# Fetches of `in` issued by POOL instead of SP, a refitted order table, and set fetches put ahead of the store in front of them

## Chip, core and metric

The kernel runs on one core of one Trainium2 chip. The metric is the device time of one execution in microseconds. The core's engines are TensorE (PE, with its weight loads PEld), VectorE (DVE), ScalarE (ACT), GpSimd (POOL) and SyncE (SP); SP only issues transfers here.

## The reference

A gated delta-rule attention is followed by two feed-forward layers (FFNs) over the same 3072 tokens:

```
for t in range(768):                       # 4 batches x 8 heads, head size 40
    y[t]  = r[t] @ state
    Sa    = state @ a[t]
    state = state * w[t] - outer(Sa, b[t]) + outer(v[t], k[t])
x   = y as (3072, 320)
x   = relu(x @ w_in)**2 @ w_out            # hidden 2048
p   = domain_probs / sum                    # 4 experts
out = sum over e of p[:, e] * (relu(x @ w1[e]) @ w2[e])   # hidden 1024 each
```

## The kernel before

**Two halves.** The first half computes the attention and the first FFN. The second half computes the four experts.

**First half.** The 768 positions are cut into 24 steps of 64, two steps to a block (12 blocks). The steps of block k are 2k (even) and 2k+1 (odd). Within a step the recurrence is solved in closed form, so that most of a step is done without the state. Its pieces, by the names that the profile shows:

- `in` (b, k and a of a step, 768 KB) is fetched by `load_in` into one of three buffers. POOL scales it in place three times (L520, L512, L520), once `P`, `q` and `s` are there (DVE). `wd`, `r`, `rf`, `v` and `xv` are smaller inputs; all fetches are issued on SP's queue.
- `pm` (PE L545, L547) multiplies a and b; ACT copies it to `mb`, SP stores that to `md` in DRAM (L563). When both steps of the block have done so, SP loads the block's matrix as `mu` (L791).
- `t` is the inverse of 32x32 triangles, 62 short instructions on DVE, each of which needs the one before it (`tmp` L808, `t` L811). Then one copy turns the layout (`mu` L818, on ACT from block 1 on), SP stores it to `td` (L823) and fetches it back transposed as `t11` and `TT` in eight transfers (L832).
- `py` (PE L679, "merge1"), `pt` (L691, "merge2"), `ptx` (L714), `px` (L637), `pys` (L726) and `pst` (L754) use the inverse and the state. DVE applies masks to `ptx` (L718, into `xv`) and adds the state to `pys` (L733, L734); POOL makes the new state `ST` and the output `y`.
- The first FFN of a block is 16 units: eight matmuls into `h` (L317), three ACT passes, one DVE pass (`gl`, L878), six matmuls into `py` of the FFN (L322 to L326). Units of an earlier block fill PE between the pieces of the recurrence.

**What sets the order there.** Every piece is an operation with an engine, a due time, its dependencies and the buffers that it takes. `Schedule.run` goes over them with a table of costs, takes on each engine the ready operation of the lowest due time, and then writes out one fixed order. Each engine runs its list in that order, and an instruction that waits holds back all that stand behind it on its engine. The due times come from `DUE` and `LEAD`; `DELAY`, `COLD` and `STAY` steer the choice; `TIMES` and `MOVE` hold the costs.

**Second half.** 96 steps on PE, one expert's quarter by one 256-token pair at a time. `Beside` hands the side work out to the steps by due step (`due`), a budget of engine time in each step, and a least distance in steps between operations that need each other on different engines (`lag`). A set is one quarter of an expert's weights: `set_load` fetches it (`wm` L1066, `wr` L1067), DVE and ACT split it into high and low parts in the buffers `w` and `z`, and `set_store` stores these to `wsd` (L1104) for a later fetch by POOL. While an expert runs, the next one's four sets are made one after the other in the same buffers. `prev` makes each set's load wait for the store of the set in front of it:

```
l = job("sp", 0.9, set_load, n, deps=prev, after=after, due=D[0])
...
if store:
    return [job("sp", 1.8, set_store, s, deps=lo, lag=0, due=D[4])]
return lo + [d]
```

Of the kernel before, what the change touches and what calls it, by code (L numbers as in the profile page):

```python
# [14 lines left out]
B, H, S, D = 4, 8, 768, 40  # L15
# [27 lines left out]
def sub(base, dims):  # L43
# [2 lines left out]

DUE = dict(block=63.76, step=[98.3, -158.9, 2.4, -355.2, -9], invert=[-219.9, -0.6, -157.6], ffn=0.2, w=[-205.6, 1.33])
LEAD = dict(  # L50
    ld_wd=894.9, ld_in=421.6, scan=77.5, m=303, t_load=135.5, t=345.2, t_out=384.9, ld_r=-259.7, ld_xv=-166,
    vm=93.4, f=84.3, kbt=47.4, x=66.9, merge=66.1, tx=131.2, ys=374.4, yq=75.2, x1=185.5,
    split=112.7,
)
DELAY = dict(PE=0.21, ACT=0, DVE=0, POOL=0, SP=0.53)


class Schedule:

    COLD = 54.3  # L60
    STAY = 20.28
    SAME = 0.033

    TILING = dict(vm=1, f=1, tx=1, x=2, ys=2, m=3, merge1=4, merge2=4)
# [1 line left out]
    AFTER = dict(l1=0.10, l2=0.12, kbt=0.12, s=0.12, tx=0.10, ys=0.10, x=0.09, vm=0.11, m=0.0, f=0.01,  # L66
                 merge1=0, merge2=0, w_pe=0.1)
    TIMES = dict(
        sq0=(.32, .38), sq1=(.32, .40), sq2=(.31, .38), sq3=(.33, .41), a_xv=(.41, .41), fx=(.38, .37), s_xv=(.335, .32),
        kbtc=(.47, .57), mc=(.42, .52), xc=(.40, .49), w_abs=(.30, .41), w_low=(.23, .35), w_hi=(.28, .38),  # L70
        t2=(.76, .76), y2=(.72, .73), fc=(.25, .35), sc=(.47, .58), tt=(.98, 1.08), x1h=(.73, .83), q1=(.30, .40),
        y1=(.31, .42), g01=(.12, .21), vmm=(.66, .70), txm=(.55, .59), rs=(.86, .93), rq=(.88, .93), P=(.62, .70),
# [2 lines left out]
        m=(.58, .65), vm=(.985, 1.12), kbt=(.41, .6), tx=(.775, .94), f=(.62, .67), merge1=(.62, .69), merge2=(.62, .69),  # L75
        s=(.44, .62), kb=(1.18, 1.25), yq=(.70, .74), scale_a=(1.22, 1.27), yf=(.41, .45), te=(.95, .9), yg=(.16, .2),
        y1d=(.28, .30),
    )
    MOVE = dict(
        ld_in=(.43, 2.85, 1.67), ld_r=(.42, .94, 1.45), ld_rf=(.45, .6, 1.65), ld_v=(.45, 1.0, 1.3), ld_wd=(.43, 1.08, 1.35),  # L80
        ld_xv=(1.28, .55, 1.9), mo=(.46, .33, .91), ti=(.46, .28, 1.35), tl=(.58, 1.44, 1.62), to=(.70, 1.05, 1.19),
        tx1=(.74, .35, .95), w_ld=(.45, .61, 1.65), y1o=(.45, 2.05, .69),
    )
# [1 line left out]
        DVE=("P", "t", "x1l", "sq", "w_clamp", "w_shift", "w_sign", "w_pow", "w_mul"),  # L85
        POOL=("scale_a", "kb", "yq", "yf", "y1d", "yg"),
# [19 lines left out]
    def run(self):  # L106
# [37 lines left out]
        while len(order) < len(ops):  # L144
            best = None
            for eng in self.ENGINES:
                first, found = 1e18, []
                for n, t in ready[eng].items():
                    t = earliest(n, t, eng, first + DELAY[eng])
                    if t is not None:  # L150
                        first = min(first, t)
                        found.append((t, n))
                if found and (best is None or first < best[0]):
                    due = lambda n: ops[n][2] + (self.STAY if eng == "PE" and self.TILING.get(n[0], 0) != tiling else 0)
                    _, n, t = min((due(n), n, t) for t, n in found if t <= first + DELAY[eng])
                    best = first, n, t
# [5 lines left out]
            if eng == "PE":  # L162
# [27 lines left out]
class Beside:  # L190
# [77 lines left out]
def tile_delta_rule_moe(  # L268
# [15 lines left out]
    pe, act, dve, pool, sp = nc.tensor, nc.scalar, nc.vector, nc.gpsimd, nc.sync  # L284
# [44 lines left out]
    op = sch.op  # L329
# [77 lines left out]
    def attention(s, tt):  # L407
        k, hb = divmod(s, 2)
        d = st[s] = {}
        T, S, f, sd = TT[hb], SS[hb], FF[hb], ST[hb]  # L410
        last = s + 2 >= nsteps
        both = lambda *n: [(x, s, h) for x in n for h in range(2)]
        o = lambda *x: x[:1] + (s,) + x[1:]
# [22 lines left out]

        def load_in():
            d["in"] = ap3.tile([128, 8, 192], F32, tag="in", name=f"in{s}")
            sp.dma_start(d["in"], kba[s])

        def load_w():
            if s == 1:
# [20 lines left out]
        def load_xv():  # L463
# [4 lines left out]
        one = lambda tag, bufs, rel, alt: [(alt, 1, rel) if s == 1 else (tag, bufs, rel)]  # L468
        op(o("ld_wd"), "SP", load_w, tt - LEAD["ld_wd"], [], prev=("ld_wd", s - 1), lat=2.7,
           alloc=one("wd", 1, [o("P", 1)], "xl"))  # L470
        op(o("ld_in"), "SP", load_in, tt - LEAD["ld_in"], [], prev=("ld_in", s - 1), lat=4.3,
           alloc=[("in", 3, both("kbt", "m") + [o("vm")] + [o("a_xv", h, j) for h in range(2) for j in range(2)])])
        op(o("ld_r"), "SP", load_r, tt - LEAD["ld_r"], [], prev=("ld_r", s - 1), lat=2.7, alloc=[("r", 1, [o("vm")])])
        op(o("ld_rf"), "SP", load_rf, tt - LEAD["ld_xv"], [], prev=("ld_rf", s - 1), lat=2.7, alloc=[("rf", 2, [o("f")])])
# [306 lines left out]
    mdd, x1 = {}, {}  # L781
# [202 lines left out]
    items = [divmod(i, NF1) for i in range(units, NF1 * nblk)]
    ffn = []
# [329 lines left out]
    job = plan.job  # L1315
    NP = NF1 + 2

    done = {}
    for P in range(NPAIR):
        k, e = 2 * P, NPW * P  # L1320
        D = {0: (-50, -15, -13, -12, -10, -7, -8, -4, -2, 0, 1), 1: (-11, -9, -10, -8, -1, 1, 1, 3, 4, 5, 5)}.get(
            P, tuple(e + d for d in (-7, -5, -5, -4, -1, -3, -2, -1, 0, -1, 0)))
# [34 lines left out]
        job("sp", 0.45, x_store, P, 6, 7, deps=b6 + [("st", P, 0)], due=e + 5, key=("st", P, 6))  # L1357

    def prepare(s, D, after, rnd, store, prev, single=False):
        n = s.n  # L1360
        l = job("sp", 0.9, set_load, n, deps=prev, after=after, due=D[0])
        w = [job(rnd, 0.36, set_round2, s, i, deps=[l], lag=2, due=D[2], after=s.free) for i in range(2)]
        lo = [job("dve", 0.41, set_low2, s, i, deps=w[i:i + 1], due=D[4]) for i in range(2)]

        def part(x, y, deps, due, after, lag=1):
            r = [job(rnd, 0.05 + (y - x) / 960, set_round, s, c, x, y, deps=deps, due=due[0], after=after, lag=lag) for c in range(2)]
            q = job("dve", 0.07 + (y - x) / 960, set_rest, s, x, y, deps=r[1:], due=due[1])
            lows = [(max(x, a), min(y, b)) for a, b in ((0, 384), (384, 768), (768, 896)) if max(x, a) < min(y, b)]
# [12 lines left out]
        return lo + [d]

    homes, spare = list(range(NPW)), NPW
    prev = []
    for n in range(NPW):
        s = Set(n, homes[n], 3 * homes[n] + 4 - NP)
        D = ((-14, -18, -10, -9, -7), (-9, -10, -4, -2, -2), (-8, -5, 2, 2, 1), (-7, -1, 1, 1, 2))[n]
        prepare(s, D, -NP - 1, ("dve", "act"), False, [], True)
    for e in range(NE - 1):
        for i in range(NPW):  # L1390
            n = NPW * (e + 1) + NPW - 1 - i
            b = PER * e + (4 if e == 0 else 0) + 5 * i
            prev = prepare(Set(n, spare, b), tuple(b + d for d in ((0, 8, 8, 8, 8) if e else (-2, 0, 5, -7, 0))), b, ("act",), i < NPW - 1, prev)
# [3 lines left out]
    for G in range(NPAIR, NE * NPAIR):  # L1397
        e, i = divmod(G, NPAIR)
# [4 lines left out]
    i = -NP  # L1403
# [131 lines left out]
```

## Time and profile before

| | us |
|---|---|
| three runs | 1464.42, 1474.74, 1477.5 |
| their median | 1474.74 |
| profiled execution, whole | 1474.95 |
| its span in the trace | 1473.2 |
| PE busy | 1381.4 (94%) |
| DVE busy | 1082.5 (73%) |
| ACT busy | 785.1 (53%) |
| POOL busy | 207.8 (14%) |

The span is the time from the first to the last instruction in the trace; 1.75 us of the execution lie around it. Busy times are sums over instructions; where PE's matmuls overlap, the union is counted. The granted clock of PE is given as a share of 2.4 GHz: 1.00 is that level, and a stretch in which it was partly at the other level (1.2 GHz) shows a value in between.

### The profile page before, as it was taken

What the parts mean: (1) busy time and instruction counts of PE and PEld (TensorE: products, weight loads), DVE (VectorE), ACT (ScalarE), POOL (GpSimd) and SP (SyncE); (2) the same over time, 40 slices, a digit from 0 to 9 for tenths busy, and PEclk for the clock granted to TensorE, in tenths of its full rate; (3) what the DMA queues carried; (4) which work ended last, traced back from release to release, by engine and by line L of the source; (5) the groups of instructions that cost most, each with busy time, mean ns of one, the idle gap of its engine ahead of it and who ended that gap; (6) DMA issues with size and microseconds to landing.
All of it is one profiled execution on the core that took longest, in us unless ns stands there. A gap on an engine that the chain in (4) does not pass through costs nothing.

```text
span 1473.2 us, 39713 instructions
## 1 busy us (share of the span) xinstructions
PE 1381.4 (94%) x16072; PEld 1312.5 (89%) x16072; DVE 1082.5 (73%) x2664; ACT 785.1 (53%) x1933; POOL 207.8 (14%) x327
## 2 busy tenths in 40 slices
PE   4698999989999999999989999999999999999998
PEld 3476888888888888898989999999999999999998
DVE  7889868778788687686648556667667776866665
ACT  5486767777777676686667445533223333322221
POOL 4120311312312312221000000100001000010000
PEclk9989989999999899998999999999999999999999
DMA  8465342442543433433142344565435244344220
GB/s 248 112 196 173 91 119 63 135 124 68 136 127 74 124 110 102 119 81 80 27 150 92 117 182 172 196 224 229 154 141 200 80 190 183 125 131 168 112 93 37
DMA packets 154679, 194.61 MB, mean 132 GB/s; under 512 B 97536, under 2 KB 118272, under 8 KB 152192
## 3 DMA queue, kind: packets, MB, share of 16 engines
q1 hardware_dynamic: 147584, 140.76, 31.2%
q0 software_dynamic: 6912, 51.32, 9.5%
q8 instruction: 127, 2.08, 0.6%
q14 instruction: 56, 0.46, 0.1%
HBM read 138.35 MB, written 48.96 MB: 127 GB/s over the span
## 4 chain that ended last, share of the span: by engine, by line
PE 60%; DVE 12%; DMA 12%; ACT 7%; SPq 4%; issue 3%; POOL 1%; DVEq 0%; ACTq 0%
PE pz L1295 7%; PE pz L1296 7%; PE pz L1294 7%; PE Q L1225 4%; PE h L317 4%; PE Q L1227 4%; PE Q L1228 4%; PE Q L1226 4%; DVE t L811 3%; DVE tmp L808 3%; DMA td<-mu 2%; DMA wr<-wf 2%; DVE gl L878 2%; PE px L637 2%; DMA TT<-td 2%
## 5 line engine op out<-in xcount | busy, mean ns | idle before, releaser
L1233 DVE TENSOR_TENSOR C<-C,Q 128x256 f32<-128x256 f32 (+1 forms) x432 | 181.9, 463 | 134.9 <-PE Q L1228 112.9
L1294 PE MATMUL pz<-w,z 128*128 128x320 f32 x768 | 238.0, 310 | 0.0
L1295 PE MATMUL pz<-w,z 128*128 128x320 f32 x768 | 237.6, 309 | 0.0
L1296 PE MATMUL pz<-w,z 128*128 128x320 f32 x768 | 237.5, 309 | 0.0
L317 PE MATMUL h<-xh,w 128*128 128x256 f32 x960 | 199.1, 290 | 0.0
L1239 ACT ACTIVATE z<-C 128x512 fp32r<-128x512 f32 x144 | 91.2, 633 | 166.7 <-DVE C L1233 164.6
L317 PE MATMUL h<-xl,w 128*128 128x256 f32 x576 | 164.3, 286 | 0.6 <-DVE xl L933 0.6
L317 PEld LDWEIGHTS h<-xh,w 128*128 128x128 f32 x960 | 158.0, 193 | 2.3
L878 DVE TENSOR_TENSOR gl<-r,gh 128x256 fp32r<-128x256 f32 x192 | 89.7, 467 | 79.4 <-ACT r L875 61.4
L1225 PE MATMUL Q<-X,w 128*128 128x256 f32 x504 | 141.5, 281 | 4.2 <-ACT C L1244 4.2
L1294 PEld LDWEIGHTS pz<-w,z 128*128 128x128 f32 x768 | 144.6, 188 | 0.0
L1295 PEld LDWEIGHTS pz<-w,z 128*128 128x128 f32 x768 | 144.5, 188 | 0.0
L1296 PEld LDWEIGHTS pz<-w,z 128*128 128x128 f32 x768 | 144.2, 188 | 0.0
L1226 PE MATMUL Q<-X,w 128*128 128x256 f32 x504 | 141.4, 281 | 0.0
L1228 PE MATMUL Q<-X,w 128*128 128x256 f32 x504 | 141.4, 280 | 0.0
L322 PE MATMUL py<-w,gh 128*128 128x320 f32 x384 | 127.1, 338 | 4.8 <-ACT gh L873 4.8
L1244 ACT COPY C<-Q 128x256 f32<-128x256 f32 x72 | 26.8, 372 | 178.0 <-PE Q L1228 178.0
L1227 PE MATMUL Q<-X,w 128*128 128x256 f32 x432 | 121.2, 281 | 0.0
L323 PE MATMUL py<-w,gh 128*128 128x320 f32 x384 | 117.9, 315 | 0.0
L317 PEld LDWEIGHTS h<-xl,w 128*128 128x128 f32 x576 | 111.6, 194 | 0.8 <-DVE xl L933 0.8
L870 ACT ACTIVATE r<-h 128x256 f32<-128x256 f32 x192 | 73.0, 380 | 62.6 <-PE h L317 54.9
L326 PE MATMUL py<-w,gl 128*128 128x320 f32 x384 | 94.0, 327 | 11.9 <-DVE gl L878 11.5
(145 smaller groups left out, 3494.5 us busy)
## 6 DMA issues: line engine op xcount, KB each, us to landing
X<-xsd POOLq DMA_DIRECT2D x12, 2688.0 KB, 9.9
in<-kba SPq DMA_DIRECT2D x24, 768.0 KB
wsd<-w SPq DMA_DIRECT2D x27, 640.0 KB
w<-wsd POOLq DMA_DIRECT2D x27, 640.0 KB, 6.9
xsd<-X SPq DMA_DIRECT2D x6, 2304.0 KB
raw<-wm SPq DMA_DIRECT2D x32, 234.0 KB
wm<-wf SPq DMA_DIRECT2D x13, 512.0 KB
wd<-w SPq DMA_DIRECT2D x24, 264.0 KB
```

The source lines that it names most:

```text
L317: pe.matmul(ps, a, b, start=n == 0, stop=n == len(mm) - 1)
L322: pe.matmul(pys[tt], gh[:, sl], t[:, 256:576], start=first, stop=False)
L323: pe.matmul(pys[tt], gh[:, sl], t[:, 960:1280], start=False, stop=False)
L878: dve.tensor_tensor(g["gl"], g["r"], g["gh"].bitcast(F32), ALU.subtract)
L1225: pe.matmul(o, hi, x[:, 0], start=True, stop=False)
L1226: pe.matmul(o, hi, x[:, 2], start=False, stop=False)
L1227: pe.matmul(o, v.low(i), x[:, 0], start=False, stop=False)
L1228: pe.matmul(o, c, x[:, 1], start=False, stop=True)
L1233: plus = lambda o, x, y: dve.tensor_tensor(o, x, y, ALU.add)
L1294: pe.matmul(py2[0][t], gh[:, sl], hi, start=j == f == 0, stop=False)
L1295: pe.matmul(py2[0][t], gh[:, sl], lo, start=False, stop=False)
L1296: pe.matmul(py2[0][t], gl[:, sl], hi, start=False, stop=j == NPW - 1 and f == 1)
```

## The change

`load_in` is issued by POOL (`pool.dma_start`) and is an operation of POOL in the schedule, with a cost in `TIMES` instead of `MOVE`. All due times, leads and four constants of the choice (`DELAY` of PE and SP, `COLD`, `STAY`) have new values, so the order of the first half changes on all engines. In the second half `prepare` passes two lists on: the load of a set needs only the set in front to be split (with `lag=0`), and the operations that write the set's buffers need that set's store. The first operations of a set that is summed have `lag=3` in place of 2.

```diff
-DUE = dict(block=63.76, step=[98.3, -158.9, 2.4, -355.2, -9], invert=[-219.9, -0.6, -157.6], ffn=0.2, w=[-205.6, 1.33])
+DUE = dict(block=65.44, step=[13, -84.1, -55.9, -383.3, 7.9], invert=[-180.9, -18.8, -282.6], ffn=21.3, w=[-102.7, 1.12])
...
-DELAY = dict(PE=0.21, ACT=0, DVE=0, POOL=0, SP=0.53)
+DELAY = dict(PE=0.32, ACT=0, DVE=0, POOL=0, SP=2.42)
...
-            sp.dma_start(d["in"], kba[s])
+            pool.dma_start(d["in"], kba[s])
...
-        op(o("ld_in"), "SP", load_in, tt - LEAD["ld_in"], [], prev=("ld_in", s - 1), lat=4.3,
+        op(o("ld_in"), "POOL", load_in, tt - LEAD["ld_in"], [], prev=("ld_in", s - 1), lat=4.3,
...
     def prepare(s, D, after, rnd, store, prev, single=False):
+        prev, kept = prev
         n = s.n
-        l = job("sp", 0.9, set_load, n, deps=prev, after=after, due=D[0])
-        w = [job(rnd, 0.36, set_round2, s, i, deps=[l], lag=2, due=D[2], after=s.free) for i in range(2)]
+        l = job("sp", 0.9, set_load, n, deps=prev, lag=0, after=after, due=D[0])
+        w = [job(rnd, 0.36, set_round2, s, i, deps=[l] + kept, lag=2 if single else 3, due=D[2], after=s.free) for i in range(2)]
...
-            r = [job(rnd, 0.05 + (y - x) / 960, set_round, s, c, x, y, deps=deps, due=due[0], after=after, lag=lag) for c in range(2)]
+            r = [job(rnd, 0.05 + (y - x) / 960, set_round, s, c, x, y, deps=deps + kept, due=due[0], after=after, lag=lag) for c in range(2)]
...
         if store:
-            return [job("sp", 1.8, set_store, s, deps=lo, lag=0, due=D[4])]
-        return lo + [d]
+            kept = [job("sp", 1.8, set_store, s, deps=lo, lag=0, due=D[4])]
+        return lo + [d], kept
```

From block 2 on, both orders repeat from block to block, with the same work in a block (60 operations on PE, 115 on DVE). Three places follow; the digits at a name's end are its step or block and a buffer number.

SP's queue where block 6's inverse goes out and comes back and block 7's matrix follows, before:

```order
L823 DMA td6_7283<-mu6_6569 64x16x32 x2
L450 DMA r14_7351<-rv 128x512
L454 DMA rf15_7353<-rv 128x512
L461 DMA v14_7364<-rv 128x512
L832 DMA t1112_7390<-td6_7283 32x256 x2
L832 DMA TT0_89<-td6_7283 32x8x32 x2
L832 DMA t1113_7408<-td6_7283 32x256 x2
L832 DMA TT1_90<-td6_7283 32x8x32 x2
L446 DMA wd17_7464<-w 128x528
L439 DMA in16_7489<-kba 128x1536
L563 DMA md7_6990<-mb15_7460 32x8x32 x4
L791 DMA mu7_7618<-md7_6990 64x1024 x2
```

and now:

```order
L823 DMA td6_7330<-mu6_6508 64x16x32 x2
L454 DMA rf15_7359<-rv 128x512
L832 DMA t1112_7365<-td6_7330 32x256 x2
L832 DMA TT0_89<-td6_7330 32x8x32 x2
L832 DMA t1113_7428<-td6_7330 32x256 x2
L832 DMA TT1_90<-td6_7330 32x8x32 x2
L446 DMA wd17_7497<-w 128x528
L563 DMA md7_6998<-mb15_7475 32x8x32 x4
L791 DMA mu7_7557<-md7_6998 64x1024 x2
L450 DMA r14_7605<-rv 128x512
L461 DMA v14_7608<-rv 128x512
```

The fetches of `r14` and `v14` stood between the store of `td6` and its eight fetches and now stand behind `mu7`; `in16` is gone from in front of the store of `md7`, and POOL issues it right behind its third scaling of `in15`, ahead of its first of `in16`.

DVE between the even and the odd step of block 6 (`xv13` are the four masks of the odd step's `ptx`, `tmp7` and `t7` the first of block 7's inverse), before:

```order
L734 TENSOR_TENSOR ys12_7651<-pys12_7620,FF0_91 128x4x64
L718 TENSOR_TENSOR xv13_6753<-ptx13_0_7672,cs_74 64x4x104 x2
L808 TENSOR_TENSOR tmp7_0_7716<-mu7_7618,t7_7285 128x31
L718 TENSOR_TENSOR xv13_6753<-ptx13_1_7673,cs_74 64x4x104
L811 TENSOR_TENSOR t7_7285<-t7_7285,tmp7_0_7716 128x31
L718 TENSOR_TENSOR xv13_6753<-ptx13_1_7673,cs_74 64x4x104
L808 TENSOR_TENSOR tmp7_1_7741<-mu7_7618,t7_7285 128x30
L733 TENSOR_TENSOR ys13_7743<-pys13_7719,ST1_94 128x4x40
L734 TENSOR_TENSOR ys13_7743<-pys13_7719,FF1_92 128x4x64
L811 TENSOR_TENSOR t7_7285<-t7_7285,tmp7_1_7741 128x30
```

and now:

```order
L734 TENSOR_TENSOR ys12_7652<-pys12_7622,FF0_91 128x4x64
L808 TENSOR_TENSOR tmp7_0_7704<-mu7_7557,t7_7332 128x31
L811 TENSOR_TENSOR t7_7332<-t7_7332,tmp7_0_7704 128x31
L808 TENSOR_TENSOR tmp7_1_7714<-mu7_7557,t7_7332 128x30
L718 TENSOR_TENSOR xv13_6754<-ptx13_0_7682,cs_74 64x4x104
L811 TENSOR_TENSOR t7_7332<-t7_7332,tmp7_1_7714 128x30
L718 TENSOR_TENSOR xv13_6754<-ptx13_0_7682,cs_74 64x4x104
L808 TENSOR_TENSOR tmp7_2_7731<-mu7_7557,t7_7332 128x58
L718 TENSOR_TENSOR xv13_6754<-ptx13_1_7683,cs_74 64x4x104
L811 TENSOR_TENSOR t7_7332<-t7_7332,tmp7_2_7731 128x29x2
```

Three of the inverse's 62 instructions now stand ahead of the odd step's first mask, where none did, and the rest of that inverse follows one place earlier. On PE, in the same block, the FFN unit that stood between `py12` and `pt12` now stands ahead of `pm15`, `pst12` stands ahead of `ptx13` instead of behind it, and `px14` of the next block's even step is issued five FFN units earlier (right behind `pst13`).

SP's queue in the second half from the load of set 11 to the load of set 10 (`wsd` are the four stores of set 11), before:

```order
L1066 DMA wm11_15562<-wf 128x2x512
L1067 DMA wr11_15563<-wf 128x640
L1193 DMA xsd_13041<-X0_5_15097 128x768
L1104 DMA wsd_13042<-w9_1172 128x1280
L1104 DMA wsd_13042<-w10_1361 128x1280
L1104 DMA wsd_13042<-w11_1548 128x1280
L1104 DMA wsd_13042<-z1_13527 128x128
L1066 DMA wm10_15942<-wf 128x2x512
L1067 DMA wr10_15943<-wf 128x640
```

and now:

```order
L1066 DMA wm11_15562<-wf 128x2x512
L1067 DMA wr11_15563<-wf 128x640
L1193 DMA xsd_13041<-X0_5_15097 128x768
L1066 DMA wm10_16006<-wf 128x2x512
L1067 DMA wr10_16007<-wf 128x640
L1104 DMA wsd_13042<-w9_1544 128x1280
L1104 DMA wsd_13042<-w10_1738 128x1280
L1104 DMA wsd_13042<-w11_1821 128x1280
L1104 DMA wsd_13042<-z1_13527 128x128
```

The load of set 10 went ahead of the four stores of set 11. The same holds for sets 9, 8, 14, 13 and 12.

## Rows read from the trace of the kernel before

**Rows 1.** Windows of the span: length, busy time of each engine, PE's granted clock, DMA.

```profile
0.00:209.00 209.00, 162.60 (x2366) 136.24 (x2366) 180.44 (x565) 140.38 (x409) 52.77 (x73) 0.93 0.55 157
...
209.00:723.00 514.00, 480.66 (x7894) 442.44 (x7896) 400.22 (x1060) 367.77 (x978) 115.03 (x178) 0.95 0.38 102
...
1040.00:1073.00 33.00, 30.20 (x220) 30.00 (x219) 21.23 (x47) 7.55 (x15) 0.54 (x1) 0.95 0.46 171
```

**Rows 2.** Line L818 on ACT: count, ns min/median/max, first and last start.

```profile
L818 ACT COPY mu<-t x11: 1070/1083/1093, 139.8 to 713.2; 128x512 f32<-128x512 f32 x11
```

**Rows 3.** Windows from `py` of the even to `ptx` of the odd step.

```profile
437.10:447.30 10.20, 10.20 (x249) 9.05 (x249) 7.16 (x14) 5.34 (x15) 3.92 (x6) 1.00 0.53 143
...
551.60:565.50 13.90, 12.69 (x250) 11.37 (x250) 7.34 (x13) 5.18 (x13) 4.59 (x7) 0.75 0.51 134
```

**Rows 4.** Timeline of DVE: start, length, instruction, idle before and releaser.

```profile
448.26 1.21 DVE L718 TENSOR_TENSOR xv<-ptx,cs 64x416 f32<-64x416 f32 x2 [1.98 <-PE ptx L714]
...
450.42 0.20 DVE L808 TENSOR_TENSOR tmp<-mu,t 128x31 f32<-128x31 f32 x1 [0.95 <-DMA mu<-md]
...
482.93 0.17 DVE L811 TENSOR_TENSOR t<-t,tmp 128x16 f32<-128x16 f32 x1
...
573.28 1.99 DVE L602 TENSOR_TENSOR xv<-pv,cs 64x512 f32<-64x512 f32 x3
...
575.43 0.69 DVE L602 TENSOR_TENSOR xv<-pv,cs 64x512 f32<-64x512 f32 x1
```

**Rows 5.** Timeline of SP's issues, blocks 7 and 8: start, length, transfer.

```profile
543.46 2.17 SPq L823 DMA_DIRECT2D td<-mu  x2
...
547.77 0.80 SPq L832 DMA_DIRECT2D t<-td  x2
...
552.92 0.38 SPq L439 DMA_DIRECT2D in<-kba  x1
...
553.39 1.87 SPq L563 DMA_DIRECT2D md<-mb  x4
...
558.54 1.14 SPq L791 DMA_DIRECT2D mu<-md  x2
```

**Rows 6.** Chain of waits, all of the span: start, length, what.

```profile
72.79 2.11 DMA TT<-td
...
166.39 1.64 DMA md<-mb
...
440.42 4.63 DMA md<-mb
...
445.74 4.66 DMA mu<-md
...
549.09 3.90 DMA TT<-td
...
1047.81 13.79 DMA wr<-wf
```

**Rows 7.** Timeline of PE, block 7.

```profile
574.82 0.63 PE L754 MATMUL pst<-cs,ST 128*128 128x128 f32 x4
```

**Rows 8.** Waits: engine, line, for what; total us, times, longest.

```profile
PE py L679 <- DMA TT<-td: 20.7, 13, 5.0
```

**Rows 9.** DMA issues on the page: transfer, queue, count, size, us to landing.

```profile
X<-xsd POOLq DMA_DIRECT2D x12, 2688.0 KB, 9.9
```

**Rows 10.** Timeline of POOL, blocks 7 and 8.

```profile
547.21 1.30 POOL L512 TENSOR_TENSOR in<-in,q 128x512 f32<-128x512 f32 x1
...
557.79 1.19 POOL L520 TENSOR_TENSOR in<-in,P 128x512 f32<-128x512 f32 x1 [9.28 <-DMA in<-kba]
...
563.50 0.45 POOL L743 TENSOR_TENSOR ST<-ys,g 128x160 f32<-128x160 f32 x1 [3.12 <-DVE ys L733]
```

**Rows 11.** Timeline of PE, second half: the first matmuls after two idle times.

```profile
1062.83 0.43 PE L1225 MATMUL Q<-X,w 128*128 128x256 f32 x1 [2.80 <-ACT C L1244]
...
1229.28 0.38 PE L1225 MATMUL Q<-X,w 128*128 128x256 f32 x1 [1.37 <-ACT C L1244]
```

More of the change, by code (lines that the diff above doesn't have):

```diff
@@ L44, in sub @@
     return AP(base.tensor, base.offset, [list(base.ap[0])] + dims)
-DUE = dict(block=63.76, step=[98.3, -158.9, 2.4, -355.2, -9], invert=[-219.9, -0.6, -157.6], ffn=0.2, w=[-205.6, 1.33])
+DUE = dict(block=65.44, step=[13, -84.1, -55.9, -383.3, 7.9], invert=[-180.9, -18.8, -282.6], ffn=21.3, w=[-102.7, 1.12])
 LEAD = dict(
-    ld_wd=894.9, ld_in=421.6, scan=77.5, m=303, t_load=135.5, t=345.2, t_out=384.9, ld_r=-259.7, ld_xv=-166,
-    vm=93.4, f=84.3, kbt=47.4, x=66.9, merge=66.1, tx=131.2, ys=374.4, yq=75.2, x1=185.5,
-    split=112.7,
+    ld_wd=755, ld_in=249, scan=57.5, m=148.3, t_load=55.6, t=203.7, t_out=640.5, ld_r=-321.9, ld_xv=30.2,
+    vm=93.4, f=70.8, kbt=49.8, x=137.4, merge=77.9, tx=141.9, ys=358.3, yq=187.2, x1=658.3,
+    split=205.4,
 )
-DELAY = dict(PE=0.21, ACT=0, DVE=0, POOL=0, SP=0.53)
+DELAY = dict(PE=0.32, ACT=0, DVE=0, POOL=0, SP=2.42)
 class Schedule:
-    COLD = 54.3
-    STAY = 20.28
+    COLD = 56.2
+    STAY = 20.24
     SAME = 0.033
@@ L68 @@
     TIMES = dict(
-        sq0=(.32, .38), sq1=(.32, .40), sq2=(.31, .38), sq3=(.33, .41), a_xv=(.41, .41), fx=(.38, .37), s_xv=(.335, .32),
+        ld_in=(.6, 6.0),        sq0=(.32, .38), sq1=(.32, .40), sq2=(.31, .38), sq3=(.33, .41), a_xv=(.41, .41), fx=(.38, .37), s_xv=(.335, .32),
         kbtc=(.47, .57), mc=(.42, .52), xc=(.40, .49), w_abs=(.30, .41), w_low=(.23, .35), w_hi=(.28, .38),
@@ L79 @@
     MOVE = dict(
-        ld_in=(.43, 2.85, 1.67), ld_r=(.42, .94, 1.45), ld_rf=(.45, .6, 1.65), ld_v=(.45, 1.0, 1.3), ld_wd=(.43, 1.08, 1.35),
+        ld_r=(.42, .94, 1.45), ld_rf=(.45, .6, 1.65), ld_v=(.45, 1.0, 1.3), ld_wd=(.43, 1.08, 1.35),
         ld_xv=(1.28, .55, 1.9), mo=(.46, .33, .91), ti=(.46, .28, 1.35), tl=(.58, 1.44, 1.62), to=(.70, 1.05, 1.19),
@@ L1379, in prepare @@
         if store:
-            return [job("sp", 1.8, set_store, s, deps=lo, lag=0, due=D[4])]
-        return lo + [d]
+            kept = [job("sp", 1.8, set_store, s, deps=lo, lag=0, due=D[4])]
+        return lo + [d], kept
     homes, spare = list(range(NPW)), NPW
-    prev = []
+    prev = [], []
     for n in range(NPW):
@@ L1387, in tile_delta_rule_moe @@
         D = ((-14, -18, -10, -9, -7), (-9, -10, -4, -2, -2), (-8, -5, 2, 2, 1), (-7, -1, 1, 1, 2))[n]
-        prepare(s, D, -NP - 1, ("dve", "act"), False, [], True)
+        prepare(s, D, -NP - 1, ("dve", "act"), False, ([], []), True)
     for e in range(NE - 1):
```

## Prediction

> **What bounds the kernel now.** I read the windows first. From 0 to 209 us DVE is the fullest engine (180.4 of 209). From 209 to 723, nine blocks of 57.1 us (514 / 9), PE is busy for 480.7 of 514 at a mean clock of 0.95 [rows 1]. The second half is full on PE but for a few idle times such as the one in the 33 us window from 1040. The turn copy, once per block, agrees on the period: (713.2 - 139.8) / 10 = 57.3 [rows 2].
>
> PE's share does not say what sets the 57.1, since it has no idle time in the one window between `py` and `ptx` and 1.2 in the other [rows 3]. So I follow what must pass once in each block. Two loops close in about that time.
>
> Loop 1 goes through the state: even `py` to odd `ptx`, odd masks, rest of the inverse, turn, `td`, fetch back, next `py`. From `py` to `ptx` it is 10.2 us at full clock and 13.9 at a mean clock of 0.75 [rows 3]; of the ten such windows from 209 on, six are like the second. The first mask starts 0.96 after `ptx` (447.30 to 448.26), and from there the inverse ends at 483.10, less the 0.95 that DVE waited for `mu`: 33.9 [rows 4]. The turn is 1.1. From the first issue of `td` to that of `t11` it is 547.77 - 543.46 = 4.3 [rows 5], and to the first `py` at 551.60 another 3.8. Sum at low clock 13.9 + 1.0 + 33.9 + 1.1 + 4.3 + 3.8 = 58.0; at full clock 54.3.
>
> Loop 2 goes through the matrix, since SP's queue keeps the store of `md` behind the fetch back: first `tmp` to last `t` 32.7 (450.42 to 483.10), turn 1.1, `td` 4.3, the eight fetches, `wd` and `in` until the first `md` issue 553.39 - 547.77 = 5.6 [rows 5], `md` to its landing 1.4 (the last of four issues) + 4.6 [rows 6], `mu` to the next `tmp` 0.5 + 4.7. Sum 54.9. In the full-clock block of rows 4, DVE waits for `mu`: there loop 2 ended last. Six blocks of 58.0 and four of 54.9 make a mean of 56.8, against the measured 57.1; so I trust the two loops.
>
> **The change part by part.**
>
> *Loads off the fetch back (loop 1).* `r` and `v` (256 KB each) no longer stand between `td` and its fetches; `rf` does. The `TT` that the chain shows took 3.9; at the start, with no fetch ahead, one took 2.1 [rows 6]. I take 1.0 off loop 1, bounds 0 and 1.8.
>
> *`in` off SP (loop 2).* Its issue slot goes: 553.39 - 552.92 = 0.5. Its 768 KB no longer lie in the queue ahead of `md`, whose landing took 4.6 behind `in` and 1.6 where none was ahead [rows 6]. But the bytes still move: after its third scaling at 548.5 POOL issues `in16`, so that transfer runs beside the fetch back and perhaps into `md`. I take the middle, 1.4 + 2.9 = 4.3, bounds 3.0 and 6.0.
>
> *DVE's order.* Three instructions of the inverse move ahead of the mask into idle time of 2.0 [rows 4], which takes 0.6 off loop 1 (33.9 to 33.3). In loop 2 more masks now lie inside the inverse: two of 0.6 (half of the 1.21 for two), 32.7 to 33.9.
>
> *PE's order.* The eight `h` matmuls of an FFN unit leave the stretch from `py` to `ptx`; `pst` (0.6, [rows 7]) enters it, and the copy of `pt` that the unit had covered is now waited for. I set them nearly equal, -0.1 (bounds -0.5 and +0.5). The unit goes ahead of `pm15`, so `pm` is later by its length, which loop 2 does not feel, since `md` waits for SP's turn behind the fetch back.
>
> After: loop 1 is 13.8 + 1.0 + 33.3 + 1.1 + 4.3 + 2.8 = 56.3 at low clock, 52.6 at full; loop 2 is 33.9 + 1.1 + 4.3 + 5.1 + 4.3 + 5.2 = 53.9. The low clock follows idle PE ahead of `py` (20.7 us over 13 waits, the longest 5.0, [rows 8]); the wait gets shorter, so I count 4 to 5 low blocks in ten instead of six. Mean 0.45 x 56.3 + 0.55 x 53.9 = 55.0 against 56.8: -1.8 a block, over nine blocks -17.
>
> On what the move to another queue gives, the Trainium skill speaks against this: "DMA: Bandwidth & Descriptors", section "Issuing engines are not separate DMA queues", says that transfers from any engine end on the same 16 DMA engines and interleave, and that issuing from several engines saves the issuing time alone. By that, `md` and `TT` keep their times; this is rival A below. The same page, "Queues, rings and completion order", says that each DMA engine takes turns between queues packet by packet, by which a small `md` need not wait for all of `in`; no run here shows either for `in`.
>
> *POOL.* It has 24 more issues. What they cost POOL, the trace does not show; the nearest landing of POOL's queue is `X` (2688 KB) at 9.9 [rows 9], and `in` by SP took 557.79 - 552.92 = 4.9 [rows 10]. Behind the scaling of `in16` POOL holds the new state `ST`, which DVE's `ys` releases at 563.5 after a wait of 3.1. Issued at 548.5 and landed after 4.9 to 9.9 (553.4 to 558.4), two scalings of 1.3 end by 561.0: nothing, with 2.5 of cover. Without that cover each us delays `ST`, and `pst`, `ptx` and loop 1 with it.
>
> *Start.* DVE does the same work there, and PE's weights no longer queue behind three fetches of `in`. -3, bounds -10 and +6.
>
> *Second half.* The load of set 10 waited behind the stores and took 13.8 [rows 6]; then PE stood for 2.8, and for 1.4 at another set [rows 11]. The low clock in the 33 us window costs 0.05 x 33 = 1.7 more [rows 1]. The load now goes ahead of the stores, while the operations that write the buffers wait for the stores, and start a step later. I take -6, bounds -6 and 0. What is late next there would be the store; its reader comes several steps later.
>
> *End of the first half.* One more FFN unit is left after the last `py`: +1.
>
> Sum on the profiled execution (1474.95, which is the median within 0.2): 1474.95 - 17 - 3 - 6 + 1 = **1450**.
>
> **The rivals.**
>
> *A. Only the issue time is saved.* `TT` stays at 3.8 and `md` at 6.0: loop 1 is 57.3 at low clock, loop 2 55.6, and with six low blocks in ten the mean is 56.6, -0.2 a block and -2 in all; then -2 - 1 - 6 + 1 gives 1467. For it: no row of the first half shows a landing that a second queue shortened, and `in16` now starts right beside the fetch back. Against it: `md` took 1.6 and `TT` 2.1 without a fetch ahead, so position in the queue has weighed.
>
> *C. PE and DVE give it back.* PE is busy 480.7 / 9 = 53.4 of a block's 57.1, and part of that is low clock. If the FFN's `gl` on DVE becomes late, units stall, and a block stays near 57. Then the second half alone counts: -6 + 1, 1470.
>
> *B. Slower: `px14` stops PE.* It now stands right behind `pst13`, which ended at 575.45 [rows 7], and needs DVE's four masks of `xv`, the last of which ended at 576.12 [rows 4]. PE would wait 0.7 a block, or up to 2.7 (all four, 1.99 + 0.69) if DVE comes to them later, and all FFN units and the next `pm` queue behind it; the idle time also keeps the low clock in every block, so that loop 1 of 56.3 holds throughout. Block: 56.3 + 2.7 = 59.0 at the most, +1.9 x 9 = +17, -6 + 1 (start 0): 1487. It loses from a wait of 1.4 on (0.8 up to today's 57.1, and 5 / 9 = 0.6 for the gain elsewhere). Against it: DVE has three inverse instructions less to do between the masks.
>
> The change also might not take `in` off the path because POOL issues it late; that would show as longer waits of POOL and falls under A.
>
> **How the numbers follow.** Forecast 0.58 (own range 1436 to 1460: all loads at their lower bound take 1.3 more off loop 2, -12 in all; low clock in every block gives +12), A 0.2 (1460 to 1469), C 0.12, B 0.1 (1475 to 1487). One per cent, 15 us, is about what a measurement of this kernel can tell, as the three runs lie 13 apart. Faster by over 1% (below 1460): the forecast and a little of A, 0.62. Slower (above 1489.5): B's far end and the unseen, 0.07. Within: 0.31. The range takes in the forecast, A and C and leaves out B: 1436 to 1474.
>
> **What would show it.** Right: no `in` on SP; `md` landing 2 to 4 us and `TT` 2.1 to 3 after their issues; turn to turn near 55; fewer windows at 0.75; the wait of `py` for `TT` under 15 us in sum; the 2.8 and 1.4 idle times gone. Wrong: `md` still at 4.6 (A), waits of `gl` or `h` that grow (C), an idle time ahead of `px` (B), or POOL's `ST` released by `in` instead of `ys`.

## The result, and the profile after

The changed kernel takes 1483.41 us (median of ten runs, 1477.9 to 1489.04), the kernel before 1473.2 (ten runs, 1464.42 to 1477.86): 1.007 times as long, 95% interval 1.0051 to 1.009. Forecast were 1450 and a range of 1436 to 1474. The profiled execution is the longest of the ten (1489.04, span 1487.3), so its 14.1 us over the span of before is more than the 10 us between the medians. The median given below for e9_rv leaves out one of its seven runs, which took 3271 us.

Windows of the changed kernel, with the columns of [rows 1]:

```profile
0.00:209.00 209.00, 167.34 (x2291) 140.92 (x2292) 185.52 (x560) 136.61 (x399) 52.69 (x80) 0.91 0.53 152
209.00:723.00 514.00, 469.83 (x7791) 436.94 (x7789) 400.01 (x1029) 354.16 (x953) 123.58 (x196) 0.92 0.38 102
390.30:407.40 17.10, 12.78 (x242) 11.65 (x243) 8.56 (x18) 5.81 (x18) 4.79 (x8) 0.70 0.52 143
394.80:407.40 12.60, 12.56 (x240) 11.52 (x241) 5.81 (x13) 4.29 (x11) 4.73 (x8) 0.67 0.37 100
1060.00:1093.00 33.00, 33.00 (x254) 33.00 (x253) 25.37 (x54) 12.61 (x25) 0.53 (x1) 1.00 0.47 172
1239.60:1254.60 15.00, 15.00 (x116) 15.00 (x115) 11.69 (x25) 4.81 (x11) 0.00 (x0) 1.00 0.58 204
```

The last two windows lie 20 us after those in which PE stood before; PE is now busy throughout. The second half gained. The loss is in the blocks: the clock of 209 to 723 fell from 0.95 to 0.92, and the stretch from even `py` to odd `ptx`, 10.2 or 13.9 in [rows 3], takes 17.1: PE is idle for 4.3, and the 12.6 behind that run at 0.67.

The turn copy on ACT, as in [rows 2]:

```profile
L818 ACT COPY mu<-t x11: 1080/1082/1089, 137.5 to 731.4; 128x512 f32<-128x512 f32 x11
```

(731.4 - 137.5) / 10 = 59.4, against 57.3. From here on I count only the nine periods from block 2's turn to block 11's: 57.0 before, 58.5 after.

What the 4.3 us of idle time wait for stands in PE's timeline of one block (block 5's turn starts at 382.6):

```profile
390.37 0.21 PE L679 MATMUL py<-TT,m 32*32 32x32 f32 x2
394.84 1.06 PE L679 MATMUL py<-TT,m 32*32 32x32 f32 x30 [4.25 <-DMA TT<-td]
...
407.40 0.94 PE L714 MATMUL ptx<-x,TT 64*64 64x104 f32 x32
```

The first `TT` is there at 390.4, 7.8 us after the turn (before, `py` started 9.4 after it in the mean); the second is not there until 394.8. In the chain of waits (start, length, what), its transfer reads like this from block to block:

```profile
269.93 6.17 DMA TT<-td
...
328.57 6.65 DMA TT<-td
...
388.81 5.98 DMA TT<-td
...
506.28 6.59 DMA TT<-td
...
687.44 1.96 DMA TT<-td
```

Before it was 3.9 in the row shown [rows 6], 3.3 to 4.3 in the chain's other blocks from block 2 on. The last row is the block in which no further `in` is fetched: 1.96. SP's and POOL's timelines of block 5 show what runs beside it:

```profile
387.49 0.81 SPq L832 DMA_DIRECT2D t<-td  x2
388.35 0.91 SPq L832 DMA_DIRECT2D TT<-td  x2
...
392.54 3.07 SPq L563 DMA_DIRECT2D md<-mb  x4
396.94 1.15 SPq L791 DMA_DIRECT2D mu<-md  x2
```

```profile
387.06 1.48 POOL L512 TENSOR_TENSOR in<-in,q 128x512 f32<-128x512 f32 x1
388.48 0.60 POOL L439 DMA_DIRECT2D in<-kba  x1
394.74 1.16 POOL L520 TENSOR_TENSOR in<-in,P 128x512 f32<-128x512 f32 x1 [5.66 <-DMA in<-kba]
...
405.00 0.45 POOL L743 TENSOR_TENSOR ST<-ys,g 128x160 f32<-128x160 f32 x1 [7.87 <-DVE ys L733]
```

POOL issues `in` at 388.48, in the middle of the fetches; `in` and the second `TT` land at the same moment, 394.7 and 394.8. `md` is stored from 392.5 and `mu` fetched at 396.9, 4.4 later where it was 5.2 [rows 5]: that part came as forecast. The sums of the waits:

```profile
POOL in L439 <- ACT kbt L614: 142.1, 8, 18.6
...
PE py L679 <- DMA TT<-td: 35.5, 13, 4.8
```

PE's wait for `TT` rose from 20.7 [rows 8] to 35.5. Of the ten heads from block 2 on (a head is the work from even `py` to odd `ptx`), eight ran at a mean granted clock under 0.9; before, it was six. The other row is POOL standing in front of the odd step's fetch until a buffer is free; behind it, `ST` still waited for DVE (7.87 above), not for this.

SP in the second half: the load now goes out ahead of the stores.

```profile
1072.80 0.38 SPq L1066 DMA_DIRECT2D wm<-wf  x1
1073.28 0.42 SPq L1067 DMA_DIRECT2D wr<-wf  x1
1073.74 1.44 SPq L1104 DMA_DIRECT2D wsd<-w  x3
```

By stage (profiled executions; turn of block 2, turn of block 11, last `py` of the FFN, end), before 200.0, 713.2, 793.2, 1473.2, after 205.0, 731.4, 812.8, 1487.3: start +5.0, nine blocks +13.2, end of the first half +1.4, second half -5.5; sum +14.1.

### The profile page after: what moved, and what is told of

Same layout as the page of the kernel before. It is cut to its first block, busy times and chain, and to the rows that moved or that the text cites. A ratio compares the mean times of both kernels' runs of the same rounds, so it can differ in the third digit from the quotient of the medians.

```text
span 1487.3 us, 39782 instructions
## 1 busy us (share of the span) xinstructions
PE 1392.5 (94%) x16072; PEld 1327.7 (89%) x16072; DVE 1097.6 (74%) x2664; ACT 781.7 (53%) x1933; POOL 215.7 (15%) x351
## 3 DMA queue, kind: packets, MB, share of 16 engines
q0 software_dynamic: 10368, 70.19, 13.2%
## 4 chain that ended last, share of the span: by engine, by line
PE 62%; DVE 17%; DMA 9%; SPq 5%; issue 4%; ACT 3%; POOL 1%; ACTq 0%; DVEq 0%; POOLq 0%
PE pz L1295 8%; PE pz L1296 7%; PE pz L1294 7%; PE Q L1227 4%; PE Q L1228 4%; PE Q L1226 4%; PE Q L1225 4%; DVE tmp L808 4%; DMA TT<-td 4%; DVE t L811 4%; PE h L317 3%; SPq L919 3%; DMA td<-mu 2%; PE ptx L714 2%; DVE gl L878 2%
## 5 line engine op out<-in xcount | busy, mean ns | idle before, releaser
L808 DVE TENSOR_TENSOR tmp<-mu,t 128x126 f32<-128x126 f32 (+22 forms) x372 | 108.0, 290 | 10.1 <-DMA mu<-md 3.7
L878 DVE TENSOR_TENSOR gl<-r,gh 128x256 fp32r<-128x256 f32 x192 | 82.7, 431 | 41.8 <-ACT r L875 39.9
```

What stands on the lines that cost most here:

```text
L808: dve.tensor_tensor(v["tmp"], a, b, ALU.mult)
```

## Experiments

The theory after this reading is collision: `in`, fetched beside the fetch back, delays the second `TT`, and the idle time in front of `py` takes the clock down for the rest of the head. Its rivals are the new order of PE and DVE, and POOL's queue as such.

| kernel | median us | ratio to before, 95% | turn to turn, us | first fetch, odd `ptx`, us after the turn |
|---|---|---|---|---|
| before | 1473.2 | | 57.0 | 5.4, 22.2 |
| changed | 1483.4 | 1.0051 to 1.009 | 58.5 | 5.0, 24.3 |
| e1_late | 1453.4 | 0.9831 to 0.99 | 55.0 | 5.0, 19.8 |
| e3_sp | 1468.9 | 0.994 to 0.9986 | 56.2 | 4.9, 20.2 |
| e4_oldorder | 1511.8 | 1.0225 to 1.0301 | 60.5 | 6.0, 25.9 |
| e5_second | 1467.8 | 0.9935 to 0.9985 | 57.0 | 5.4, 22.0 |
| e6_oldlate | 1482.5 | 1.0043 to 1.0096 | 58.1 | 6.2, 23.2 |
| e7_half | 1466.7 | 0.9929 to 0.9987 | 56.7 | 5.2, 22.4 |
| e8_spearly | 1482.5 | 1.0029 to 1.0083 | 58.0 | 5.3, 23.4 |
| e9_rv | 1456.3 | 0.9867 to 0.9941 | 54.9 | 5.1, 20.6 |
| e10_fill | 1467.9 | 0.9927 to 0.9974 | 56.1 | 5.3, 21.9 |
| e11_latefill | 1454.8 | 0.9847 to 0.9893 | 54.9 | 5.5, 19.1 |
| e12_oldfill | 1457.7 | 0.9877 to 0.9918 | 55.9 | 5.9, 21.1 |
| e13_oddsp | 1469.3 | 0.9909 to 0.9953 | 56.6 | 5.5, 21.6 |

The last two columns are means of nine periods, read from the starts of the turn copy, SP's issues (the first fetch back of the inverse) and PE's matmuls. Each ratio is to runs of the kernel before that were taken along with that kernel (their medians are 1472.8 to 1476.6).

**e1_late: the same order, `in` later.** Against the changed kernel, in the list that `Schedule.run` writes out:

```diff
+        for s in range(8, NSTEP, 2):
+            a = order.index(("yq", s - 4, 1))
+            for n in (("kb", s, 1), ("kb", s, 0), ("ld_in", s)):
+                order.remove(n)
+            a = order.index(("yq", s - 4, 1))
+            order.insert(a + 1, ("ld_in", s))
+            a = order.index(("scale_a", s))
+            order[a:a] = [("kb", s, 0), ("kb", s, 1)]
         for n in order:
             ops[n][1]()
```

Expected: 

> The changed kernel, but POOL issues each even step's in only after the output y of the even step of the block in front, about 20 us later, and scales it behind the odd step's y; the order of all other engines is that of the changed kernel. Collision theory (the 768 KB of in run beside the fetch back of t11 and TT, so the second TT lands 6.0 us after its issue instead of 3.9, PE stands 4.2 us and runs the head of every block at the low clock): the second TT lands in under 4, the head of the block has idle time under 2.5, turn to turn is 56 to 57 instead of 58.5 to 60, and the whole is 1452 to 1468. Order theory (the new order of PE and DVE costs the block; the transfer is harmless): turn to turn stays at 58.5 or more, whole 1478 to 1490. Queue theory (a fetch issued by POOL slows SP's transfers or POOL's own work wherever it stands): 1475 to 1490, with a loss at the new place, near the odd step.

Measured 1453.4, 30 us less than the changed kernel. POOL issues each even step's `in` 18.0 to 21.9 us after the turn, where it was 5.9 in the changed kernel: 12 to 16 us later, not 20. The turn copy, PE's wait for `TT`, three rows of the chain and one head (window):

```profile
L826 ACT COPY mu<-t x11: 1073/1081/1092, 133.3 to 696.0; 128x512 f32<-128x512 f32 x11
```

```profile
PE py L687 <- DMA TT<-td: 8.9, 11, 2.1
```

```profile
317.13 3.89 DMA TT<-td
...
430.06 3.07 DMA TT<-td
...
596.90 1.87 DMA TT<-td
```

```profile
431.60:442.90 11.30, 9.88 (x246) 8.65 (x250) 7.04 (x15) 5.80 (x17) 2.79 (x6) 1.00 0.50 111
```

`TT` takes 1.9 to 3.9, the wait falls from 35.5 to 8.9, this head runs at full clock (four of the ten are still under 0.9). Only POOL's list differs, so the order of PE and DVE is not what cost, nor POOL's queue as such. Turn to turn is 55.0, a little below what was expected of this run. The kernel beats both others.

**e4_oldorder: the old order, only the queue.** In the kernel before:

```diff
-            sp.dma_start(d["in"], kba[s])
+            pool.dma_start(d["in"], kba[s])
```

Expected: 

> The kernel before with its order and its second half; only load_in is issued by POOL, which puts each even step's in right behind the third scaling of the odd step, as in the changed kernel. Collision theory: the second TT lands 5 to 6 us after its issue, the idle time ahead of py grows, turn to turn 58.5 to 59.5, whole 1483 to 1495. Order theory: PE and DVE keep the old order, so turn to turn is 57 or, with md sooner, 55 to 56, whole 1458 to 1474.

Measured 1511.8, worse than collision was given. From the chain:

```profile
269.08 6.00 DMA TT<-td
...
330.28 6.27 DMA TT<-td
```

Turn to turn rises by 3.5 (57.0 to 60.5), where 1.5 to 2.5 were expected. But not all of it is the collision at the fetch back: the odd step's `in`, too, now goes out by POOL, and runs beside the store of `td` (see e6_oldlate below), so the first fetch is issued at 6.0 instead of 5.4. The early issue of the even step's `in` alone, against a late one, costs 3.5 us a block in the new order (58.5 against 55.0 in e1_late) and 2.3 in the old one (60.5 against 58.1 in e6_oldlate).

What the new order is worth depends on where `in` goes out: 0.9 a block with all of it on SP (57.0 to 56.2, e3_sp), 2.0 with POOL's early fetches (60.5 to 58.5), 3.1 with the late ones (58.1 to 55.0).

**e3_sp: the new order, `in` on SP at its old place.**

```diff
-            pool.dma_start(d["in"], kba[s])
+            sp.dma_start(d["in"], kba[s])
...
+        for s in range(8, NSTEP, 2):
+            order.remove(("ld_in", s))
+            order.insert(order.index(("mo", s - 1, 0, 0)), ("ld_in", s))
```

Expected: 

> The changed kernel with its order, but in is issued by SP, each even step's in at the place that it had before (behind the fetch back and wd, ahead of the store of md). Collision theory: the second TT is back at 3 to 4 us, md behind in is slow again (landing over 4), turn to turn about 57; with the slower start (+5) and the faster second half (-5.5) the whole is 1465 to 1474. Order theory: turn to turn stays at 58.5 or more, 1478 to 1490.

1468.9, as collision expected. Its five periods from block 2 on are 55.1 to 55.7, the last three full ones 57.6, 60.7 and 58.9. In the middle one of these DVE waited for `mu` (timeline), which stands behind `in` again:

```profile
561.56 0.20 DVE L811 TENSOR_TENSOR tmp<-mu,t 128x31 f32<-128x31 f32 x1 [4.63 <-DMA mu<-md]
```

Why the period grows in the later blocks only stays open.

**e7_half and e8_spearly: how many bytes, and whose queue.** e7_half leaves the first half of each even step's `in` at the early place and moves the second; e8_spearly has SP issue all of it right ahead of the fetch back:

```diff
...
+                pool.dma_start(d["in"][:, 0:4], kba[s][:, 0:4])
+                sch.rest[s] = lambda: pool.dma_start(d["in"][:, 4:8], kba[s][:, 4:8])
...
```

```diff
-            pool.dma_start(d["in"], kba[s])
+            sp.dma_start(d["in"], kba[s])
...
+        for s in range(8, NSTEP, 2):
+            order.remove(("ld_in", s))
+            order.insert(order.index(("ti", s // 2 - 2, 0, 0, 0)), ("ld_in", s))
```

Expected of e7_half: 

> The changed kernel with half of each even step's in (384 KB) issued by POOL at the early place and the other half late; scalings late as in e1_late. Collision by bytes: the second group of py comes about halfway between 10.4 us after the turn (e1_late) and 12.6 (changed kernel), turn to turn 56 to 57.5, whole 1462 to 1475. If what hurts is that any fetch of POOL runs there (its issue, its descriptors, not its bytes): as the changed kernel, 1478 to 1488. If only the last part of in hurt: as e1_late, 1450 to 1458.

Expected of e8_spearly: 

> The changed kernel with each even step's in issued by SP right ahead of the four first fetches of t11 and TT, so that the same bytes move at the same moment in the same queue as the fetch back. Collision by moment and bytes: second group of py at 12 or later after the turn, turn to turn 58 or more, whole 1476 to 1495. If POOL's queue beside SP's is what hurts and the same bytes ahead in one queue do not (as r, rf and v, 768 KB as well, stood there in the kernel before): second group of py near 11, turn to turn 56, whole 1462 to 1472.

Half the bytes cost about half: 1466.7, turn to turn 56.7. The third matmul of the even step's `py`, the one that waits for the second `TT` in the changed kernel, starts 10.3 us after the turn in the mean (9.1 in e1_late, 12.0 in the changed kernel; the 10.4 and 12.6 in the expectation do not agree with the starts in the traces). In its chain:

```profile
379.32 4.74 DMA TT<-td
...
436.50 4.05 DMA TT<-td
```

With SP the same bytes at the same moment cost as much as with POOL, 1482.5, turn to turn 58.0. The wait has another form: behind `in` in one queue the first `TT` is late as well, so PE stands ahead of all 32 matmuls of `py` and not behind the second. The third starts at 11.1, less late than the 12 expected. The chain, and PE's timeline of one block:

```profile
325.59 4.33 DMA TT<-td
...
383.48 5.26 DMA TT<-td
```

```profile
388.88 1.12 PE L682 MATMUL py<-TT,m 32*32 32x32 f32 x32 [3.88 <-DMA TT<-td]
```

So it is the moment and the bytes; the queue makes no difference to the time that shows.

**e10_fill, e11_latefill, e12_oldfill: wait or clock.** Ahead of the even step's `py`, PE gets idle matmuls (nine in the changed kernel, three in e1_late, four in e5_second); `py` overwrites what they write:

```diff
                 py = d["py"] = psa.tile([128, 8, 32], F32, tag="at", name=f"py{s}")
+                for _ in range(9 if s >= 4 and s % 2 == 0 else 0):
+                    pe.matmul(py.rearrange("p a x -> p (a x)"), ident, cs[:, 0:256], start=True, stop=True)
```

Expected of e10_fill: 

> The changed kernel with nine idle matmuls (128x128 on 128x256, some 0.43 us each at full clock, 3.9 us in all) ahead of the even step's py in blocks 2 to 11, written into py's own bank and overwritten there; they do no work of the reference and fill the time in which PE waits for the second TT. Theory idle-then-clock (the late TT costs its wait, and the wait costs the clock of the head that follows, 12.5 us for what takes 9 to 10 at full clock): the head runs at full clock in most blocks, its end comes 2 to 3 us earlier, turn to turn is 56 to 57, whole 1460 to 1470. If the head is slow for another reason (its order, the DMA traffic, the clock falling whatever PE does): turn to turn stays at 58.5 or grows, 1480 to 1500.

Expected of e11_latefill: 

> e1_late with three such idle matmuls (1.3 us) ahead of the even step's py. Idle-then-clock: the blocks with a slow head (about four of nine) become like the others, turn to turn 54 to 54.7, whole 1444 to 1451. Otherwise PE comes up to 1.3 us later to py, and the whole is 1453 to 1463.

Expected of e12_oldfill: 

> e5_second (old first half) with four such idle matmuls (1.7 us) ahead of the even step's py. Idle-then-clock: the six slow heads of ten turn fast, turn to turn 55 to 56, whole 1450 to 1460 against 1468. Otherwise 1466 to 1480.

e10_fill: 1467.9, so 15.5 us of the loss are back, although `TT` lands as late as before. Chain, PE's timeline and the head of block 5 (window):

```profile
384.16 5.25 DMA TT<-td
```

```profile
385.76 3.40 PE L677 MATMUL py<-cs 128*128 128x256 f32 x15
389.09 1.05 PE L681 MATMUL py<-TT,m 32*32 32x32 f32 x32
```

```profile
389.00:399.20 10.20, 10.01 (x247) 8.66 (x250) 5.33 (x13) 4.36 (x12) 4.69 (x8) 1.00 0.56 135
```

The head is 10.2 at clock 1.00; in the changed kernel the same work from 394.8 to 407.4 took 12.6. Of the ten heads, one is under 0.9, where eight were. Of the 3.5 us that the collision cost a block, 2.4 (58.5 to 56.1) come back with the clock; the rest goes with the wait, which is as long as it was (the third matmul of `py` starts 12.1 after the turn, 12.0 in the changed kernel). The old first half gains as well, 1467.8 to 1457.7; its window

```profile
209.00:723.00 514.00, 488.93 (x8161) 445.96 (x8158) 404.25 (x1069) 373.28 (x996) 114.85 (x178) 1.00 0.39 102
```

is at 1.00, 0.95 before. e11_latefill missed: the clock of its blocks rose to 1.00 too and the odd `ptx` comes sooner (19.1 after the turn, 19.8 in e1_late), but 1454.8 is no gain over e1_late, and turn to turn stays at 54.9. There loop 2 ends last in most blocks; DVE stands ahead of the inverse until `mu` is there (waits: us in sum, times, longest; 4.0 in sum in the kernel before, 19.2 in e1_late):

```profile
DVE tmp L818 <- DMA mu<-md: 26.9, 8, 4.1
```

**e5_second: the second half alone.** The kernel before with the new `prepare`.

Expected: 

> The kernel before with the second half of the changed kernel alone (set fetches ahead of the stores). All theories: the two idle times of 2.8 and 1.4 us and the low clock behind them go, whole 1467 to 1469 (5.5 less); first half as before. If the second half's gain in the changed kernel came from its different entry and not from this: 1473, and the idle times stay.

1467.8, ratio 0.996, as forecast; PE's idle times are gone (windows):

```profile
1040.00:1073.00 33.00, 33.00 (x253) 33.00 (x253) 25.58 (x54) 12.38 (x25) 0.54 (x1) 1.00 0.46 172
1220.00:1235.00 15.00, 15.00 (x115) 15.00 (x115) 11.51 (x25) 4.99 (x11) 0.00 (x0) 1.00 0.57 203
```

**e6_oldlate and e13_oddsp: the queue move without the new order.** e6_oldlate is e5_second with `in` on POOL and the list edit of e1_late. e13_oddsp gives the odd steps' fetch back to SP:

```diff
-            pool.dma_start(d["in"], kba[s])
+            (sp if s % 2 and s > 8 else pool).dma_start(d["in"], kba[s])
```

Expected of e6_oldlate: 

> The kernel before with the faster second half, in on POOL and each even step's in issued late, as in e1_late; the order of the other engines is the old one. If the gain of e1_late over the kernel before comes from the queue move alone (in off SP, at a harmless moment), turn to turn is 55 as there and the whole 1450 to 1456. If the new order brings it and the queue only takes in out of loop 2, which is not the longer loop in blocks at low clock, turn to turn is 56.3 to 57 and the whole 1460 to 1468.

Expected of e13_oddsp: 

> e6_oldlate (old order, faster second half, even steps' in late by POOL), but the odd steps' in from step 9 on is issued by SP again, at its old place in SP's queue ahead of the store of td. If e6_oldlate lost because POOL's odd in runs beside td: the first fetch comes at 5.3 us after the turn again instead of 6.0, turn to turn is 57 or less, whole 1458 to 1470. If the late even in on POOL is what costs in the old order: turn to turn stays at 58, whole 1476 to 1486.

e6_oldlate missed both expectations: 1482.5. In the old order POOL's odd fetch goes out about 1.3 us ahead of the turn and runs beside the store of `td`; SP's went out 2.0 ahead of it. The store in the chain of e6_oldlate, then of e13_oddsp (4.3 and 3.6 in the mean of nine blocks):

```profile
494.67 4.23 DMA td<-mu
```

```profile
496.52 3.35 DMA td<-mu
```

e13_oddsp came out as the first branch of its expectation has it: first fetch at 5.5 instead of 6.2, turn to turn 56.6, 1469.3. That is no better than e5_second (1467.8): in the old order, moving the even steps' `in` to POOL brings nothing that shows, even at a harmless moment.

**e9_rv: `r` and `v` back in front of the fetch back**, on top of e1_late:

```diff
+        for k in range(2, 11):
+            for n in (("ld_v", 2 * k + 2), ("ld_r", 2 * k + 2)):
+                order.remove(n)
+                order.insert(order.index(("to", k, 1)) + 1, n)
```

Expected: 

> e1_late with r and v back in their old place, between the store of td and its fetches. If their issues on SP cost (0.6 and 0.4 us, with the queue behind them), the first fetch starts 1.0 to 1.5 later and turn to turn is 56 to 56.5, whole 1462 to 1468. If SP waits for td anyway and only the bytes count, the first fetch starts as in e1_late, TT lands up to 1 us later, and the whole is 1453 to 1462.

1456.3 against 1453.4, intervals that overlap, and turn to turn 54.9 against 55.0: no difference that shows, as the second branch of the expectation has it. SP waits for `td` anyway. From the store of `td` to the first fetch it takes 3.8 in e1_late and 3.9 in e9_rv (SP's timelines, e1_late first):

```profile
424.91 1.38 SPq L831 DMA_DIRECT2D td<-mu  x2
...
428.74 0.81 SPq L840 DMA_DIRECT2D t<-td  x2
```

```profile
423.00 1.37 SPq L835 DMA_DIRECT2D td<-mu  x2
...
426.88 0.81 SPq L844 DMA_DIRECT2D t<-td  x2
```

(The mean of 5.1 in the table comes from one block at 6.2; the others are at 4.9 to 5.0.) The bytes do count: the third matmul of `py` starts 9.7 after the turn instead of 9.1, and the odd `ptx` comes 0.8 later. Loop 1 had that much room.

That the first fetch is sooner in the new order than in the kernel before (5.0 instead of 5.4) is due to the store itself, not to `r` and `v`. In the chain of the kernel before, then of the changed kernel, it takes:

```profile
430.03 3.43 DMA td<-mu
```

```profile
384.40 3.08 DMA td<-mu
```

In most blocks this goes with the moment of the odd step's `in`: 3.1 where that is issued 3.5 us or more ahead of the turn (by POOL in the changed kernel and e1_late, by SP in e3_sp), 3.4 to 3.7 at 2.0 ahead (before), 4.1 to 4.5 at 1.3 ahead (e6_oldlate). It is not the whole cause: in a few late blocks of e7_half, e9_rv, e10_fill and e11_latefill the store took up to 4.5 with `in` issued 3.6 ahead, and why stays open.

## Why the prediction was wrong

- **What bounds the kernel** held as far as the runs go: a late `TT` lengthens the block (loop 1), and where `TT` is early DVE stands for `mu` (loop 2, e3_sp and e11_latefill). That a block without the collision takes 55.0, the figure that the prediction reached, is in part luck. Its 55.0 is a mean of 56.3 at low clock and 53.9 at full clock; e11_latefill has all its heads at full clock and takes 54.9.
- **The step that failed** is *Loads off the fetch back (loop 1)*, "I take 1.0 off loop 1, bounds 0 and 1.8". The next paragraph says that `in16` "runs beside the fetch back", but no price was put on it, and the bounds end at no loss. `TT` went from 3.9 to 6.0 (chain). The count of low-clock blocks, forecast to fall from six to four or five, hangs on the same wait: that did not get shorter but rose from 20.7 to 35.5, and eight heads of ten ran at low clock. The collision costs 3.5 a block (55.0 in e1_late, 58.5 here), which is more than the 2.0 that e1_late gains on the kernel before: the nine blocks took (58.5 - 57.0) x 9, from the unrounded periods +13.2, in place of -17. With `in` out of the way, in e1_late, the third matmul of `py` does start 1.0 sooner than before (9.1 after the turn, 10.1 before), as much as the 1.0 that the step took.
- *`in` off SP*: from the first issue of `md` to that of `mu` it takes 4.4 in the mean where it had been 5.4, in the direction forecast. e3_sp and e1_late differ by this (6.2 and 4.7) and by the wait of DVE for `mu`: 56.2 and 55.0 us a block.
- *`r` and `v`*: the prediction counted their bytes, and rightly: put back, they delay the third matmul of `py` by 0.6 (e9_rv against e1_late). The other 0.4 of the 1.0 is the first fetch, which is sooner by that much as the store of `td` is shorter (see e9_rv); the prediction did not look at that. e9_rv also shows that the time does not need `r` and `v` moved.
- *DVE's and PE's order*: the new order saves 0.9 to 3.1 a block, by where `in` goes out. No run divides that between DVE, PE and the loads.
- *Start*, -3: +5.0 in this profile. But e1_late, e7_half and e9_rv, which do not differ from the changed kernel up to that point, reach the turn of block 2 at 200.8, 199.6 and 200.2, about as before (200.0); e10_fill and e11_latefill, which do not either, reach it at 203.9 and 204.4. So one order gives 199.6 to 205.0 from execution to execution, and the +5.0 of one profile is no sign of a slower start. The -3 was not there in any profile.
- *Second half*, -6: -5.5, and e5_second shows it alone. *End of the first half*, +1: +1.4.
- The sum has two slips that change nothing here: nine times -1.8 is -16, not -17, and the middle of the bounds 3.0 and 6.0 for `md` is 4.5, not 4.3.
- **Rivals.** A kept `TT` and `md` at their old lengths, and C and B put the trouble on PE and DVE; none had a transfer made slower. DVE's masks stopped PE in front of `px` once in the whole span, for 0.6 (waits), so B did not come true. POOL's `ST` still waits for `ys`, as forecast.
- The Trainium skill's "DMA: Bandwidth & Descriptors", section "Issuing engines are not separate DMA queues", says that transfers interleave on the same engines whoever issues them. The runs agree: 1483.4 with POOL, 1482.5 with SP at the same moment. From the section "Queues, rings and completion order" of that page of the Trainium skill, by which each DMA engine takes turns between queues packet by packet, the prediction drew that a small transfer need not wait for all of a large one in another queue. Here 32 KB beside 768 KB landed after 6.0 us, with it and not ahead of it, and after 1.96 in the block without `in`; whether the engines took turns in between, no run shows.

## What to carry to other kernels

A fetch that is moved to another queue is moved to another moment: list what short transfers of the critical loop are under way then, and price the delay of those by the bytes beside them, with a bound that allows a loss. Where PE waits in front of a chain of small matmuls, price the wait and the clock of the work behind it together; here the clock was 2.4 of the 3.5 us that a block lost, and idle matmuls in the wait gave it back. If a move loses, try the same list with that one issue elsewhere before dropping it: the changed kernel with `in` issued 12 to 16 us later is the fastest of all, 1453.4.

## What the runs showed of the hardware

- Idle matmuls in a wait of 4 us kept the granted clock at 1.00 for the head behind it (in nine heads of ten; two in the changed kernel). In the windows shown, a head behind a wait had 0.67 to 0.75 without them. Nine of them a block were worth 15.5 us in the changed kernel and four of them 10 in the old first half; three were worth nothing in e1_late, where loop 2 ended last.
- 768 KB beside two 32 KB fetches stretched the later one to 4.9 to 6.7 us (1.96 in the block without, 1.9 to 3.9 in e1_late). Half the bytes, from POOL, gave 3.1 to 4.8; all of them from SP ahead in the same queue 3.3 to 5.7 (rows of the chain).
- The store of `td` took 4.3 us in the mean with a 768 KB fetch of POOL's issued 1.3 us ahead of the turn (e6_oldlate), and 3.6 with the same fetch issued by SP 2.0 ahead of it (e13_oddsp).
